# One feature block of the second token group moved from plain to paired products, in a fused retention and feed-forward kernel

## The chip, the cores and the metric

The kernel runs on one core of a Trainium2 chip. The metric is the device time of one execution in microseconds (us); the median of several runs is compared. Beside the runs there is one profiled execution, whose trace gives every instruction's start and length on each engine: PE (TensorE; PEld is its loading of stationary operands), DVE (VectorE), ACT (ScalarE), POOL (GpSimd) and SP (SyncE, which only issues transfers here).

## The reference

The input of the feed-forward part is the output of a retention block: four sequences of 768 tokens, eight heads of 64.

```python
for t in range(S):
    state = gamma * state + einsum('bhd,bhe->bhde', k[:, :, t], v[:, :, t])
    y[:, :, t] = scale * einsum('bhd,bhde->bhe', q[:, :, t], state)
x = y.transpose(0, 2, 1, 3).reshape(3072, 512)
h = x @ w_in                                   # 512 x 2048
sp = maximum(h, 0) + log1p(exp(-abs(h)))       # softplus
out = (h * erf(sp)) @ w_out                    # 2048 x 512
```

The weights arrive as 64-bit floats and are read as pairs of 32-bit words.

## The kernel before

**Tiling.** The 3072 tokens are 24 chunks of 128 (`j`), two chunks make a group of 256 (`g`, 12 of them). x of a group, transposed, is `XC[g]`: 128 partitions, 4 parts of the 512 features, 256 tokens. The 2048 hidden features are 16 blocks of 128 (`ft`), w_in comes in 8 pieces `n` of two blocks, w_out in 8 pieces as well.

**Two ways to multiply.** A *plain* product (`hidden_of`, L694) is one fp32 product of a block with one group, 4 parts deep; each shows as two matmuls of 256 columns. It needs only the converted weight. A *split* product multiplies in a rounded format: weight and x are each split into three tiles hi, lo, dif (`split_weights`, `split_x`), and three matmuls take the place of one. `unit(g, n)` (L728) does a piece's two blocks for one group, 256 columns each; `pair_unit(g, ft)` (L762) does one block for groups g and g+1 at once, 512 columns. Its sums lie in two PSUM banks `a` and `b`, which are weighted and joined: by ACT and DVE (`together`, L340 and L341), or, for the pair of groups 1 and 2 (`APART`), both are only scaled by ACT (L773, L774), stored as a high and a low part (`HID3`), and added on DVE when they are loaded again (`add_lows`, L913).

**Who is done how.** `ALONE` gives how many blocks of a group are done without a partner group: 16 of group 0, 10 of group 1, 8 of group 11. Group 0, and blocks 0 to 9 of group 1, are plain. Blocks 10 to 15 of group 1 are paired with group 2; blocks 8 and 9 of group 2 are left over and done by `unit(2, 4)`.

**Order.** The order on each engine is written out by hand; an engine takes its instructions strictly in the order in which the program issues them.

1. The retention of chunks 0 to 3 (L796 to L837), with scores, masks, products with the state, and after each chunk `A(j)` = `ret_add`: the state addition on DVE (L543) and a copy of half of the chunk's x on ACT (L536). Between them `next(weight_steps)` does single steps of the conversion of w_in to fp32: DVE takes the exponent (L235), ACT scales it (L238), DVE joins the mantissa's words (L249, L254), sets the sign (L258) and multiplies (L270). When a piece is through, its buffer is loaded again (`load_piece`, and for the first two pieces `load` of a later chunk). `need("in", ft)` does steps until block ft is converted. PE is given `keep_warm` products of the unit matrix where it would idle.
2. A loop over ft (L863): `hidden_of(ft, 0)`, `hidden_of(ft, 1)` while ft < `ALONE[1]`, the conversion two or three blocks ahead, then the items of the list `during` (the retention of chunks 4 and 5: `begin`, `states`, `results`, `crossed_sums`; splits), then `put_hidden(ft)`, which copies a bank of plain results to SBUF (ACT, L705 or L708) and stores it (POOL's queue). The plain banks are two buffers named `hp`.
3. Periods g = 2 to 11 (L1075), each a list of units with items between them: two more chunks of retention (`joined`: `begin` before one unit, `results` before another), weights split, the next chunks prepared, w_out converted in `convert` steps. `LOADS` says after which units of a period a quarter of a raw piece of w_out is loaded (POOL's queue; two buffers, so a third piece waits for the first one's last read, L258).
4. The projection (L1098): hidden values are loaded again (`load_hidden`, SP's queue), softplus, erf and product, split, and multiplied with w_out (L977). Each step n has 48 matmuls, 10.9 us.

Of the kernel before, what the change touches and what calls it, by code (L numbers as in the profile page):

```python
# [13 lines left out]
F32 = mybir.dt.float32  # L14
# [3 lines left out]
AF = mybir.ActivationFunctionType  # L18
# [3 lines left out]
P = 128  # L22
C = 128
JPC = 4
GT = 256
# [19 lines left out]
Z = 2.0**-12  # L45
# [4 lines left out]
def kernel(  # L50
# [23 lines left out]
    DH = d_model // 2  # L74
    FIRST = JPC // 2 - 1

    ALONE = {0: n_ft, 1: 5 * n_ft // 8, NG - 1: n_ft // 2}
    assert D == 64 and d_model == H * D and n_k == HP == 4 and S % GT == 0 and NJ % 2 == 0
    assert H == 8 and n_ft == 16 and NC > JPC and GT == 2 * C

# [11 lines left out]
    def b4(name, shape, dtype=F32):  # L92
        return big.tile([P] + shape, dtype, name=name, tag="b4")
# [334 lines left out]
    psum_turn = itertools.cycle((ps_r, ps_h))  # L428


    idle = ps_o.tile([P, P], F32, name="o0")

    def keep_warm(n):
        for _ in range(n):
            nc.tensor.matmul(idle, ident, ident, start=True, stop=True)

    keep_warm(7)

# [247 lines left out]

    def hidden_of(ft, g):

        bank, col = (ft, g) if ft < ALONE[1] else (ft - ft % 2, ft % 2)
        if bank not in HP_:  # L690
            HP_[bank] = ps_h.tile([P, 2, GT], F32, name="hp")
        w = WF[ft // 2].rearrange("p h a f -> p (h a) f")
        for kk in range(n_k):
            nc.tensor.matmul(  # L694
                HP_[bank][:, col],
                w[:, kk, ft % 2 * P : (ft % 2 + 1) * P], XC[g][:, kk],
                start=(kk == 0), stop=(kk == n_k - 1),
            )

    def put_hidden(ft):  # L700
        if ft >= ALONE[1] and ft % 2 == 0:
            return
        h = b2("h", [2, GT])
        if ft >= ALONE[1]:
            nc.scalar.copy(h, HP_.pop(ft - 1))  # L705
            nc.gpsimd.dma_start(HID[0][:, ft - 1 : ft + 1], h)
            return
        nc.scalar.copy(h, HP_.pop(ft))  # L708
        for g in range(2):
            nc.gpsimd.dma_start(HID[g][:, ft], h[:, g])  # L710
# [8 lines left out]
        names = [f"o{2 * own + i}" if pool is ps_o else "hp" if pool is ps_h else "r" for i in range(2)]  # L719
        return [pool.tile([P, 2, GT], F32, name=name) for name in names]  # L720

    def unit(g, n):

        a, b = banks(g == NG - 1)
        for to, parts in ((a, (0, 1)), (b, (2,))):
            for u in range(2):
                for kk, i in itertools.product(range(n_k), parts):
                    nc.tensor.matmul(  # L728
                        to[:, u],
                        W[n][i][:, kk * 2 * P + u * P : kk * 2 * P + (u + 1) * P],  # L730
                        X[g][i][:, kk],
                        start=(u == 0 and kk == 0 and i == parts[0]),
                        stop=(kk == n_k - 1 and i == parts[-1]),
                        skip_group_check=True,
                    )
        def put():
            if g not in ALONE:
                h = b4("h", [2, 2, GT])
                nc.scalar.activation(h[:, :, 0], a, AF.Copy, scale=1 + 1 / Z)
                nc.scalar.activation(h[:, :, 1], b, AF.Copy, scale=-1 / Z)  # L740
                for u in range(2):
                    nc.gpsimd.dma_start(HID3[FIRST][:, 2 * n - NPC + u, :, place_of(FIRST, g)], h[:, u])
                return
            h = b2("h", [2, GT])
            together(h, a, b)
            nc.gpsimd.dma_start(HID[g][:, 2 * n - NPC : 2 * n - NPC + 2], h)

        return put

    def place_of(g, of):  # L750

        return int(of % 3 > min(g % 3, (g + 1) % 3))
# [81 lines left out]
    ret_out(JPC - 1, lambda: hidden_of(0, 0), state_last=True)  # L834
    need("in", 1)
    hidden_of(1, 0)
    A(JPC - 1)  # L837


# [39 lines left out]
    def load_hidden(n):  # L879

        if n >= NG * NU:
            return
        HID_[n] = b4("hid", [4, GT])
        g, i = divmod(n, NU)
        of = g if g % 2 == i // 2 else g - 1
        LOWS[n] = []
        four, both = slice(i % 2 * 4, i % 2 * 4 + 4), FIRST <= of < NG - 1
        if of in APART:

            own = place_of(of, g)  # L890
            for f in range(2):
                at = slice(four.start + 2 * f, four.start + 2 * f + 2)
                if g == of and 8 + at.start < ALONE[g]:
                    src = HID[g][:, 8 + at.start : 8 + at.stop]
                else:
                    src = HID3[of][:, at, 0, own]
                    LOWS[n].append((f, b2("low", [2, GT])))
                    nc.sync.dma_start(LOWS[n][-1][1], HID3[of][:, at, 1, own])
                nc.sync.dma_start(HID_[n][:, 2 * f : 2 * f + 2], src)
        elif both:  # L900
            nc.sync.dma_start(HID_[n], HID2[of][:, four, place_of(of, g)])
        else:
            nc.sync.dma_start(HID_[n], HID[g][:, i * 4 : i * 4 + 4] if g < 2 else HID[g][:, four])
# [4 lines left out]

    def add_lows(k):
        for n in (2 * k, 2 * k + 1) if k < NH else ():  # L910
            for f, low in LOWS.pop(n):
                x = HID_[n][:, 2 * f : 2 * f + 2]
                nc.vector.tensor_tensor(x, x, low, op=ALU.add)  # L913

    def softplus(k):
# [87 lines left out]
        }  # L1003


    LOADS = {4: (3, 4, 5, 6), 5: range(2, 8), 6: (0, 1, 4, 5, 6, 7), 7: (2, 3, 4, 5), 8: (1, 2, 3, 4)}

    vals = values(2 * JPC)

    def period(g, prep, next_prep):  # L1010

        a, b = 2 * g + 2, 2 * g + 3
        one, two = partial(partial, unit), partial(partial, pair_unit)
        if g == G2:
            units = [one(g, 4)] + [two(1, ft) for ft in range(ALONE[1], n_ft)]
            return units, joined(3, 5, g), {
                0: [(hi_of, 6)],
                1: [(split_weights, 6)],
                2: [(hi_of, 7)],
                3: [(states, a), (states, b), (split_weights, 7)],  # L1020
                4: [(hi_of, 0), (split_weights, 0)],
                5: [(crossed_sums, a), (crossed_sums, b), (split_x, a, 2)],
                6: [(hi_of, 1), (split_weights, 1), (steps, next_prep, 1)],
            }, range(4)
        if g < NG:
            units = [two(g - 1, ft) for ft in range(8 - 8 * (g % 2), 16 - 8 * (g % 2))]
        if g == G2 + 1:
            return units, joined(3, 5, g), {
                0: [(steps, vals), (hi_of, 2), (steps, prep, 1)],
                1: [(steps, prep, 1), (steps, vals)],  # L1030
                2: [(split_weights, 2), (hi_of, 3)],
                3: [(states, a), (states, b), (split_weights, 3)],
                5: [(crossed_sums, a), (crossed_sums, b), (split_x, a, 2)],
                7: [(steps, next_prep, 1)],
            }, range(4)
        if g < NG - 2:
            return units, joined(2, 5, g), {
                0: [(steps, prep, 4)],
                1: [(convert, 2)],
                2: [(states, a), (convert, 1)],  # L1040
                3: [(states, b), (convert, 1)],
                4: [(convert, 2 if g < 8 else 1)],
                5: [(crossed_sums, a), (crossed_sums, b)],
                6: [(split_x, a, 2)],
                7: [(steps, next_prep, 1 if g < NG - 3 else 4), (convert, 1)],
            }, LOADS.get(g, ())
        if g == NG - 2:
            return units, joined(1, 3, g), {
                0: [(steps, prep, 4), (load_w_out, 0)],
                1: [(states, a), (load_w_out, 1)],  # L1050
                2: [(states, b), (split_w_out, 0)],
                3: [(crossed_sums, a), (crossed_sums, b)],
                4: [(split_w_out, 1), (load_hiddens, 0)],
                5: [(split_x, a, 2)],
                6: [(softplus, 0), (load_w_out, 2)],
                7: [(erf, 0), (gated, 0)],
            }, ()
        if g == NG - 1:
            return units, {}, {
                0: [(split_g, 0), (split_w_out, 2), (load_w_out, 3)],  # L1060
                1: [(split_g, 1), (load_hiddens, 1)],
                2: [(split_w_out, 3)],
                3: [(softplus, 1), (load_w_out, 4)],
                4: [(erf, 1)],
                5: [(split_w_out, 4), (load_w_out, 5)],
                6: [(gated, 1)],
                7: [(split_g, 2), (load_hiddens, 2)],
            }, ()
        return [one(NG - 1, n) for n in range(NPC // 2, NPC)], {}, {
            0: [(split_w_out, 5), (load_w_out, 6)],  # L1070
            1: [(split_g, 3), (load_w_out, 7)],
            2: [(split_w_out, 6)],
        }, ()
# [92 lines left out]
```

## Time and profile before

| what | us |
|---|---|
| runs, median (lowest to highest of 3) | 609.08 (608.69 to 610.02) |
| the profiled execution, its own time | 609.44 |
| its span, first to last instruction | 607.7 |
| busy in the span: PE / PEld | 601.1 / 503.4 |
| busy in the span: DVE / ACT / POOL | 463.0 / 395.1 / 132.3 |

The span has four stretches: retention of the first chunks to 26 us, plain blocks to 75.5 us, periods of units to 343 us, the projection to the end. The busiest lines of PE:

```profile
L762 PE MATMUL o<-x_hi,w_hi 128*128 128x512 f32 x296 | 117.4, 397 | 0.0
L977 PE MATMUL o<-w_hi,g_hi 128*128 128x512 f32 x120 | 46.7, 389 | 0.0
L694 PE MATMUL hp<-xT,w 128*128 128x256 f32 x208 | 46.3, 381 | 0.0
```

Read: line, engine, operation, result and operands, size of the stationary operand and of the result, how many, then busy time in us, the mean length of one in ns, and the engine's idle time before them. A matmul's length reaches to its modelled end and overlaps the next one; the distance between starts is what it costs when PE is fed. The mean granted TensorE clock is 0.999.

### The profile page before, as it was taken

Reading aid. Unit: us, or ns where it says so; the run is one execution under the profiler, and the core shown is the slowest. Engines: PE = TensorE matmul, PEld = TensorE weight load, DVE = VectorE, ACT = ScalarE, POOL = GpSimd, SP = SyncE. Lnnn points to the kernel's source line nnn. Section 1 sums busy time; section 2 is a strip of 40 time slices with the busy share of each in tenths; the row PEclk is TensorE's granted clock in tenths of the full one; section 3 lists DMA queues with packets and bytes.
Section 4 is the critical chain, followed back from the end, with each engine's and each line's share of the span. In section 5 each row is a group of like instructions: output and inputs, shape, how many; then the busy total and the mean of one; then the engine's idle time right before and its main releaser. Section 6 shows DMA issues by size and latency. Waiting matters only on the chain.

```text
span 607.7 us, 13134 instructions
## 1 busy us (share of the span) xinstructions
PE 601.1 (99%) x5174; PEld 503.4 (83%) x5174; DVE 463.0 (76%) x579; ACT 395.1 (65%) x620; POOL 132.3 (22%) x223
## 2 busy tenths in 40 slices
PE   8999999999999999999999999999999999999997
PEld 7888888888888888888888988888888888888886
DVE  5899898777978779787778995887777768668540
ACT  3684858354453544445487788889889888988920
POOL 1086563243536435242112200000000000000000
PEclk9999999999999999999999999999999999999999
DMA  9999698988969998795655937145424433531300
GB/s 201 305 279 269 159 259 249 248 183 241 244 177 292 262 261 189 240 234 157 204 161 186 306 127 236 47 133 174 138 70 139 146 103 99 173 126 48 105 35 35
DMA packets 147692, 109.93 MB, mean 181 GB/s; under 512 B 103152, under 2 KB 127472, under 8 KB 147632
## 3 DMA queue, kind: packets, MB, share of 16 engines
q1 hardware_dynamic: 131536, 59.93, 39.1%
q0 software_dynamic: 15536, 49.04, 25.4%
q8 instruction: 40, 0.66, 0.5%
q10 hardware_dynamic: 560, 0.14, 0.1%
q14 instruction: 20, 0.16, 0.1%
HBM read 71.58 MB, written 37.49 MB: 179 GB/s over the span
## 4 chain that ended last, share of the span: by engine, by line
PE 96%; SPq 2%; DMA 1%; ACT 0%; DVE 0%; issue 0%; DVEq 0%
PE o L762 34%; PE o L977 21%; PE r L977 11%; PE hp L977 11%; PE hp L694 8%; PE o L728 1%; DMA raw<-in_moe_w_in_dram 1%; PE hp L590 1%; PE hp L762 1%; PE r L762 1%; PE r L639 1%; PE hp L639 1%; PE r L590 1%; PE r L650 1%; PE r L597 1%; SPq L141 1%
## 5 line engine op out<-in xcount | busy, mean ns | idle before, releaser
L762 PE MATMUL o<-x_hi,w_hi 128*128 128x512 f32 x296 | 117.4, 397 | 0.0
L762 PE MATMUL o<-x_lo,w_lo 128*128 128x512 f32 x296 | 115.4, 390 | 0.0
L340 ACT ACTIVATE h<-o 128x512 f32<-128x512 f32 x70 | 41.5, 596 | 91.3 <-PE o L762 88.0
L932 DVE TENSOR_TENSOR e<-hid,e 128x1024 f32<-128x1024 f32 x48 | 56.6, 1222 | 55.6 <-ACT e L922 55.6
L762 PE MATMUL o<-x_dif,w_dif 128*128 128x512 f32 x296 | 79.1, 389 | 0.0
L341 DVE SCALAR_TENSOR_TENSOR h<-o,h 128x512 f32<-128x512 f32 x70 | 47.8, 687 | 30.9 <-ACT h L340 26.3
L779 POOL DMA_DIRECT2D hids<-h x72 | 39.7, 552 | 130.7 <-DVE h L341 129.7
L762 PEld LDWEIGHTS o<-x_hi,w_hi 128*128 128x128 f32 x296 | 55.5, 188 | 12.4
L762 PEld LDWEIGHTS o<-x_dif,w_dif 128*128 128x128 f32 x296 | 55.6, 188 | 11.6
L762 PEld LDWEIGHTS o<-x_lo,w_lo 128*128 128x128 f32 x296 | 55.6, 188 | 11.0
L334 DVE SCALAR_TENSOR_TENSOR g_dif<-g_hi,g_lo 128x1024 fp32r<-128x1024 f32 x48 | 58.8, 1225 | 3.3
L332 ACT ACTIVATE g_hi<-e 128x1024 fp32r<-128x1024 f32 x48 | 51.0, 1063 | 14.9 <-DVE e L932 12.4
L333 DVE TENSOR_TENSOR g_lo<-e,g_hi 128x1024 fp32r<-128x1024 f32 x48 | 58.7, 1222 | 0.1
L918 ACT ACTIVATE e<-hid 128x1024 f32<-128x1024 f32 x48 | 48.4, 1054 | 0.9 <-DVE hid L913 0.7
L922 ACT ACTIVATE e<-e 128x1024 f32<-128x1024 f32 x48 | 48.3, 1054 | 0.3
L977 PE MATMUL o<-w_hi,g_hi 128*128 128x512 f32 x120 | 46.7, 389 | 0.0
L977 PE MATMUL o<-w_lo,g_lo 128*128 128x512 f32 x120 | 46.7, 389 | 0.0
L977 PE MATMUL o<-w_dif,g_dif 128*128 128x512 f32 x120 | 46.7, 389 | 0.0
L694 PE MATMUL hp<-xT,w 128*128 128x256 f32 x208 | 46.3, 381 | 0.0
L694 PEld LDWEIGHTS hp<-xT,w 128*128 128x128 f32 x208 | 39.0, 190 | 5.3
L574 ACT ACTIVATE v<-v,kq_s 128x64 f32<-128x64 f32 x144 | 35.8, 342 | 0.0
L918 ACT ACT_TABLE_LOAD x24 | 30.8, 1283 | 3.4 <-DVE hid L913 1.9
(211 smaller groups left out, 1252.3 us busy)
## 6 DMA issues: line engine op xcount, KB each, us to landing
hids<-h POOLq DMA_DIRECT2D x72, 256.0 KB, 4.2
hid<-hids SPq DMA_DIRECT2D x36, 512.0 KB, 5.0
raw<-in_moe_w_in_dram SPq DMA_DIRECT2D x32, 256.0 KB, 5.3
raw<-in_moe_w_out_dram POOLq DMA_DIRECT2D x32, 256.0 KB, 6.3
out_dram<-y SPq DMA_DIRECT2D x23, 256.0 KB, 2.3
kb<-in_k_dram SPq DMA_DIRECT2D x144, 32.0 KB, 3.9
v<-in_v_dram POOLq DMA_DIRECT2D x18, 256.0 KB, 6.2
kn<-in_k_dram POOLq DMA_DIRECT2D x18, 256.0 KB, 6.8
```

Source lines behind the costliest of these rows:

```text
L332: nc.scalar.activation(hi, x, AF.Copy, scale=KEEP)
L333: nc.vector.tensor_tensor(lo, x, hi.bitcast(F32), op=ALU.subtract)
L334: nc.vector.scalar_tensor_tensor(dif, hi.bitcast(F32), Z, lo.bitcast(F32), op0=ALU.mult, op1=ALU.subtract)
L340: nc.scalar.activation(to, a, AF.Copy, scale=1 + 1 / Z)
L341: nc.vector.scalar_tensor_tensor(to, b, -1 / Z, to, op0=ALU.mult, op1=ALU.add)
L694: nc.tensor.matmul(HP_[bank][:, col], w[:, kk, ft % 2 * P : (ft % 2 + 1) * P], XC[g][:, kk], start=(kk == 0), stop=(kk == n_k - 1),)
L762: nc.tensor.matmul(to, W[n][i][:, kk * 2 * P + u * P : kk * 2 * P + (u + 1) * P], XR[i][:, at, kk], start=(kk == 0 and i == parts[0]), sto ...
L779: nc.gpsimd.dma_start(HID2[g][:, ft % 8], h)
L918: nc.scalar.activation(E[n], HID_[n], AF.Softplus)
L922: nc.scalar.activation(E[n], E[n], AF.Erf)
L932: nc.vector.tensor_tensor(E[n], HID_.pop(n), E[n], op=ALU.mult)
L977: nc.tensor.matmul(Y[g][t][x // 2], G[n][x][:, f, t * P : (t + 1) * P], W_OUT[ft // 2][x][:, ft % 2 * d_model : (ft % 2 + 1) * d_model], s ...
```

## The change

It does five things. `ALONE[1]` becomes 9, so block 9 of group 1 is paired with group 2 (`pair_unit(1, 9)`), `unit(2, 4)` keeps only its first block (`both=False`), and period g = 2 has eight units instead of seven with its items shifted by about one; `load_hidden` handles a pair of blocks of which one is plain. Two conversion steps (of piece 1) are issued ahead of `A(3)`. `keep_warm` makes one product of up to four widths of the unit matrix instead of up to four products. The quarters of raw w_out are loaded after later units (`LOADS`).

```diff
-    ALONE = {0: n_ft, 1: 5 * n_ft // 8, NG - 1: n_ft // 2}
+    ALONE = {0: n_ft, 1: n_ft // 2 + 1, NG - 1: n_ft // 2}
...
-    idle = ps_o.tile([P, P], F32, name="o0")
+    idle = ps_o.tile([P, 4, P], F32, name="o0")
...
     def keep_warm(n):
-        for _ in range(n):
-            nc.tensor.matmul(idle, ident, ident, start=True, stop=True)
+        for i in range(0, n, 4):
+            m = min(4, n - i)
+            nc.tensor.matmul(
+                idle[:, :m], ident, ident[:, None, :].to_broadcast([P, m, P]), start=True, stop=True
+            )
...
     def hidden_of(ft, g):
-        bank, col = (ft, g) if ft < ALONE[1] else (ft - ft % 2, ft % 2)
+        bank, col = (ft, g) if ft <= ALONE[1] else (ft - ft % 2, ft % 2)
...
     def put_hidden(ft):
-        if ft >= ALONE[1] and ft % 2 == 0:
+        if ft > ALONE[1] and ft % 2 == 0:
             return
         h = b2("h", [2, GT])
-        if ft >= ALONE[1]:
+        if ft == ALONE[1]:
+            nc.scalar.copy(h[:, 0], HP_.pop(ft)[:, 0])
+            nc.gpsimd.dma_start(HID[0][:, ft], h[:, 0])
+            return
+        if ft > ALONE[1]:
             nc.scalar.copy(h, HP_.pop(ft - 1))
...
-    def unit(g, n):
+    def unit(g, n, both=True):
...
-            for u in range(2):
+            for u in range(2 if both else 1):
...
             if g not in ALONE:
-                h = b4("h", [2, 2, GT])
-                nc.scalar.activation(h[:, :, 0], a, AF.Copy, scale=1 + 1 / Z)
-                nc.scalar.activation(h[:, :, 1], b, AF.Copy, scale=-1 / Z)
-                for u in range(2):
-                    nc.gpsimd.dma_start(HID3[FIRST][:, 2 * n - NPC + u, :, place_of(FIRST, g)], h[:, u])
+                h = b2("h", [2, GT])
+                nc.scalar.activation(h[:, 0], a[:, 0], AF.Copy, scale=1 + 1 / Z)
+                nc.scalar.activation(h[:, 1], b[:, 0], AF.Copy, scale=-1 / Z)
+                nc.gpsimd.dma_start(HID3[FIRST][:, 2 * n - NPC, :, place_of(FIRST, g)], h)
                 return
...
     need("in", 1)
     hidden_of(1, 0)
+    next(weight_steps)
+    next(weight_steps)
     A(JPC - 1)
...
             for f in range(2):
                 at = slice(four.start + 2 * f, four.start + 2 * f + 2)
-                if g == of and 8 + at.start < ALONE[g]:
-                    src = HID[g][:, 8 + at.start : 8 + at.stop]
-                else:
-                    src = HID3[of][:, at, 0, own]
-                    LOWS[n].append((f, b2("low", [2, GT])))
-                    nc.sync.dma_start(LOWS[n][-1][1], HID3[of][:, at, 1, own])
-                nc.sync.dma_start(HID_[n][:, 2 * f : 2 * f + 2], src)
+                k = max(0, ALONE[of] - 8 - at.start) if g == of else 0
+                if k:
+                    nc.sync.dma_start(HID_[n][:, 2 * f : 2 * f + k], HID[g][:, 8 + at.start : 8 + at.start + k])
+                at = slice(at.start + k, at.stop)
+                to = slice(2 * f + k, 2 * f + 2)
+                LOWS[n].append((to, b2("low", [2 - k, GT])))
+                nc.sync.dma_start(LOWS[n][-1][1], HID3[of][:, at, 1, own])
+                nc.sync.dma_start(HID_[n][:, to], HID3[of][:, at, 0, own])
...
-    LOADS = {4: (3, 4, 5, 6), 5: range(2, 8), 6: (0, 1, 4, 5, 6, 7), 7: (2, 3, 4, 5), 8: (1, 2, 3, 4)}
+    LOADS = {
+        4: (4, 5, 6, 7), 5: (2, 3, 4, 5), 6: (0, 1, 2, 3, 5, 6, 7), 7: (0, 3, 4, 5, 6), 8: (2, 3, 4, 5),
+    }
...
         if g == G2:
-            units = [one(g, 4)] + [two(1, ft) for ft in range(ALONE[1], n_ft)]
-            return units, joined(3, 5, g), {
+            units = [one(g, 4, False)] + [two(1, ft) for ft in range(ALONE[1], n_ft)]
+            return units, joined(4, 6, g), {
                 0: [(hi_of, 6)],
-                1: [(split_weights, 6)],
-                2: [(hi_of, 7)],
-                3: [(states, a), (states, b), (split_weights, 7)],
-                4: [(hi_of, 0), (split_weights, 0)],
-                5: [(crossed_sums, a), (crossed_sums, b), (split_x, a, 2)],
-                6: [(hi_of, 1), (split_weights, 1), (steps, next_prep, 1)],
+                2: [(split_weights, 6), (hi_of, 7)],
+                4: [(states, a), (states, b), (split_weights, 7)],
+                5: [(hi_of, 0), (split_weights, 0)],
+                6: [(crossed_sums, a), (crossed_sums, b), (split_x, a, 2)],
+                7: [(hi_of, 1), (split_weights, 1), (steps, next_prep, 1)],
             }, range(4)
```

More of the change, by code (lines that the diff above doesn't have):

```diff
@@ L910, in add_lows @@
         for n in (2 * k, 2 * k + 1) if k < NH else ():
-            for f, low in LOWS.pop(n):
-                x = HID_[n][:, 2 * f : 2 * f + 2]
+            for at, low in LOWS.pop(n):
+                x = HID_[n][:, at]
                 nc.vector.tensor_tensor(x, x, low, op=ALU.add)
```

## The prediction

> **What bounds the kernel now.** I read the totals and the chain first. TensorE (PE) is busy 99% of the span and makes up 96% of the chain that ended last.
>
> ```profile
> span 607.7 us, 13134 instructions
> PE 601.1 (99%) x5174; PEld 503.4 (83%) x5174; DVE 463.0 (76%) x579; ACT 395.1 (65%) x620; POOL 132.3 (22%) x223
> PE 96%; SPq 2%; DMA 1%; ACT 0%; DVE 0%; issue 0%; DVEq 0%
> ```
>
> A busy PE need not be a fed one, so next the chain in order of time (start, length, what).
>
> ```profile
> 11.25 5.66 DMA raw<-in_moe_w_in_dram
> ...
> 17.47 0.72 ACT power L238
> ...
> 39.46 6.91 PE hp L694 x32
> ...
> 75.86 2.87 PE o L728 x24
> 78.73 5.47 PE o L762 x24
> ```
>
> Up to 17 us a transfer of raw w_in sets the end; from about 19 us on only PE stands in the chain. The starts of PE's matmuls keep one cadence from there to 604 us: 0.216 us in plain blocks (6.91/32), 0.120 in `unit` (2.87/24), 0.227 in `pair_unit` (5.47/24, between starts a hair less). The first after a change of shape is followed about 0.1 us late. So DVE, ACT, POOL and the queues matter only where they make PE wait, and PE instructions count in full.
>
> **The change, part by part.** Durations are of the profiled execution, 609.44 us (span 607.7), which is 0.36 above the median of the runs, 609.08.
>
> *Features.* The second group's tenth block, `hidden_of(9, 1)`, goes: 4 fp32 products, two recorded matmuls each, 8 x 0.216 = -1.73. `unit(2, 4)` halves: 12 x 0.120 = -1.44. `pair_unit(1, 9)` comes: 12 x 0.227 = +2.72. Changes of shape stay as many. Together -0.44 us. [...] The trace has 0.227 in every `pair_unit`, and that row decides.
>
> *Evictions, stores and reloads.* ACT loses 2 x 0.24 on the halved `unit` (0.60 for 512 columns, 0.37 for 256) and 0.2 on block 9, and gains 2 x 0.60; POOL has the same number of stores, less one; the reload of blocks 8 and 9 of group 1 becomes three SP transfers instead of one, with one more low half of 256 columns, a DVE addition near 0.42 us (128x256 at L543). That addition has more than a projection step, 10.9 us, before PE wants its result. All zero. Without that cover each would cost its own time, 0.4 us at most.
>
> *Period g = 2.* It has eight units, not seven, and the splits and chunk steps keep their distance to the units that read them (`begin` to `results` two units, weights 6 and 7 two units before use). The new second unit wants x_lo of group 1 at about 75.6 us on the old time axis with PE's 1.73 taken off; L333 delivers it at 74.67. Zero, with 0.9 us of cover.
>
> *Raw w_out loads.* Fewer wait for a buffer that is still being read (POOL waited 8.9 us for L258 in total). Each piece is still issued four units, some 11 us, before its first step, against 6.3 us to landing. POOL's waits are not on PE's path: zero. DVE would be blocked from some 4 us of lateness on (11 less 6.3).
>
> *Dummies.* 22 recorded matmuls become 8 over the same 11 x 128 columns. The first seven products took 3.36 us, and PE then idled 0.31 until DVE was ready; the pairs are followed by an idle 0.28. A lost or gained 0.3 is hidden there, and the chain is with the DMA until 16.91 anyway. Zero, bounds -0.3 to +0.3.
>
> *Conversion steps ahead of `A(3)`.* This edit can cost. Before, `A(3)` comes first: a state addition on DVE (L543), then the copy of half of chunk 3's x on ACT (L536). DVE, then ACT:
>
> ```profile
> 24.47 0.69 DVE L270 SCALAR_TENSOR_TENSOR w<-w,power 128x512 f32<-128x512 f32 x1
> 26.35 0.42 DVE L543 TENSOR_TENSOR state<-state,o 128x256 f32<-128x256 f32 x1 [1.19 <-PE o L530]
> 26.69 0.42 DVE L235 TENSOR_SCALAR power<-raw 128x512 uint32<-128x512 uint32 x1
> 27.02 0.42 DVE L249 TENSOR_SCALAR w<-raw 128x512 uint32<-128x512 uint32 x1
> 27.48 0.69 DVE L254 SCALAR_TENSOR_TENSOR w<-w,raw 128x512 f32<-128x512 uint32 x1
> 28.09 0.42 DVE L235 TENSOR_SCALAR power<-raw 128x512 uint32<-128x512 uint32 x1
> ```
>
> ```profile
> 26.81 0.37 ACT L536 COPY xT<-o 128x256 f32<-128x256 f32 x1 [0.52 <-DVE state L543]
> 27.14 0.72 ACT L238 ACTIVATE power<-power,below 128x512 uint32<-128x512 uint32 x1
> 28.54 0.72 ACT L238 ACTIVATE power<-power,below 128x512 uint32<-128x512 uint32 x1 [0.68 <-DVE power L235]
> ```
>
> The two moved steps are the four DVE rows from L235 to the second L235 and both ACT rows L238; they issue no DMA. They fill DVE's idle 1.19 us, but L543 and L536 now queue behind them, and behind L536 stands PE: `hidden_of(0, 1)` reads this x first. It is due when `hidden_of(1, 0)`, begun at 26.23, is through: 26.23 + 0.32 + 7 x 0.216 = 28.06. DVE is free at 25.16, but piece 1's last quarter, issued at 19.88, lands 6.0 us later:
>
> ```profile
> DMA to landing us min/median/max: 6.0/6.0/6.0
> ```
>
> So at 25.92 and L235 at 26.02 (0.10 after landing, as with the first raw piece). The second L235 follows 1.40 later (26.69 to 28.09) at 27.42, its L238 0.45 later (28.09 to 28.54) at 27.87, L536 0.63 after that (one L238 of 0.72 with the overlap seen at 17.47 to 18.10), 28.50 to 28.87; PE restarts 0.03 later at 28.90. That is 0.84 late, and 0.1 at the restart makes 0.9 us. The gain of the edit is nothing: the conversions PE reads next have 1.7 us or more in hand (block 2 done at 29.83, read at 31.5). Bounds: 0, if the piece landed by 25.1, and 1.9 if a further microsecond late. I take +0.9, the row.
>
> **Sum**: -0.44 + 0.9 = +0.46 us: 609.9 against the profiled execution, 609.5 against the median. Some 0.2% (1.2 us) is what a measurement of this kernel can tell from no change, so this is no change.
>
> **Rivals.**
>
> *A, no stall.* If piece 1 lands 0.9 us sooner than in this one execution, DVE starts at 25.16, L536 ends near 28.0, PE never waits: -0.44, 608.6. For it: the landing before came at 24.15 and the following ones every 0.68 us, so 25.92 is an outlier by 1.1. Against: the next rival's rows explain the outlier by something that stays.
>
> *B, the program's own transfers move, faster.* In 14.4 to 15.7 us and again in 22 to 24.3 us the DMA view has one packet of 16 KB of another queue:
>
> ```profile
> q8 instruction: 1, 0.02, 5.5%
> ```
>
> The page has 40 of them; 10,348 PE instructions over 40 is 259 each, so they follow PE's count. The second precedes the late landing at 25.92, the first the raw transfer at 11.25 that took 5.66 us where the one before took 4.6. With 28 PE instructions fewer (14 matmuls, 14 weight loads) the first comes some 0.5 us later, past that transfer, which would land up to 1.1 us sooner. PE then waits for chunk 3's keys (landed 17.86): transposed at 18.35, copied at 18.96, scores at 19.1 instead of 19.57, 0.47 us won: -0.44 - 0.47 = -0.9, 608.2; at most -1.5. [...] Against: the second packet, 28 instructions later, waits for the state addition that ends at 22.75, and so still falls ahead of piece 1; then the stall above eats what the start won.
>
> *C, slower: ACT's copies of the plain blocks.* PE reaches blocks 10 to 15 1.73 us sooner, while ACT runs there without a gap from 64.54 us:
>
> ```profile
> 64.54 0.72 ACT L238 ACTIVATE power<-power,below 128x512 uint32<-128x512 uint32 x1 [0.89 <-DVE power L235]
> 65.17 1.04 ACT L332 ACTIVATE x_hi<-xT 128x1024 fp32r<-128x1024 f32 x1
> 66.12 0.57 ACT L708 COPY h<-hp 128x512 f32<-128x512 f32 x1
> ```
>
> Block 12 needs the bank that this L708 empties: at 66.49 with the half shape (0.37), and PE comes at 61.78 + 0.10 + 24 x 0.216 = 67.07 instead of 68.80. It decides from 0.6 us of lateness; block 14 behind L705 has 0.7. If ACT or DVE hold PE back there, the whole 1.73 is waited out: +0.46 + 1.73 = +2.2, 611.3. Against: the x they wait for comes from PE itself, so both shift together.
>
> *D, the dummies do not do it.* Fewer of them over equal columns, nothing gained or lost: this is inside the forecast.
>
> **How the numbers follow.** Forecast 0.52, A 0.20, B 0.12, C 0.16. The forecast alone: 609.0 to 610.3 (stall 0.4 to 1.4, and the runs' own scatter). The range goes to half of B below and most of the way to C above: 608.1 to 611.0. Slower by over 0.2% (above 610.3): all of C and the stall's upper end, 0.21. Faster by over 0.2% (below 607.9): the deep end of B and scatter, 0.09. Within: 0.70.
>
> **What would show it.** In the chain: L694 x200, L728 x84 in all and 12 more L762 columns of work; PE's idle time before the second eight of L694 near 28 us, ended by ACT xT L536, with L536 behind two L238; no PE wait between 62 and 76 us (else C); the first raw transfer landing before 16 us (else not B). The forecast is wrong if that wait is absent, or if any later gap of PE exceeds 0.5 us.

## The result and the profile after

| what, us | before | after |
|---|---|---|
| runs beside each other, median (lowest to highest of 22) | 609.03 (608.50 to 610.86) | 610.54 (609.23 to 619.29) |
| ratio of after to before, 95% interval | | 1.0024 [1.0017, 1.0031] |
| the profiled execution, its own time | 609.44 | 610.31 |
| its span | 607.7 | 608.3 |
| start of PE's last matmul | 603.72 | 603.93 |

The changed kernel is slower by 0.24%, some 1.5 us: just over what can be told from no change. The prediction was 609.5 and no change; the measured 610.54 lies 1 us above, inside its range of 608.1 to 611.0 but above the 609.0 to 610.3 of its forecast alone, and part of its reasons fail. Single executions far above the others of their kernel (619.29 here, 1009.58 of after_merged and 621.21 of features_dummies below) are disturbed; they are in no ratio, and no time is read from their traces.

Totals and chain of the changed kernel, then its plain blocks, the first of its `unit` rows and of its `pair_unit` rows (line, engine, operation, names, shapes, how many | busy us, mean ns | idle before). Line 694 before is L698 now, 728 is L736, 762 is L769, 590 and 597 are L594 and L601.

```profile
span 608.3 us, 13092 instructions
PE 600.6 (99%) x5152; PEld 500.4 (82%) x5152; DVE 463.1 (76%) x580; ACT 395.0 (65%) x622; POOL 131.3 (22%) x222
PE 96%; SPq 2%; DMA 1%; issue 0%; ACT 0%; DVE 0%; DVEq 0%
```

```profile
L769 PE MATMUL o<-x_hi,w_hi 128*128 128x512 f32 x300 | 118.9, 396 | 0.0
...
L698 PE MATMUL hp<-xT,w 128*128 128x256 f32 x200 | 44.6, 381 | 0.0
L736 PE MATMUL o<-x_hi,w_hi 128*128 128x256 f32 x20 | 5.1, 292 | 0.0
```

The work is what the prediction counted: 8 plain matmuls fewer (208 to 200), four of each kind of `unit` fewer (24 to 20), four of each kind of `pair_unit` more (296 to 300). PE is busy 0.5 us less, yet the execution is 0.9 us longer. So something other than work was added; totals can't show it, but the distance between the same events of both traces does.

| at | after minus before, us | what came in between |
|---|---|---|
| start of the burst at 50.6 us | -0.28 | the start |
| start of the burst at 84 us | -0.73 | the features: -0.45 |
| start of the burst at 131 us | -1.03 | before's burst at 115 us lasted 0.3 us longer |
| start of the burst at 183 us | -1.03 | nothing |
| end of that burst | +0.34 | it lasts 3.39 us instead of 2.02 |
| last matmul | +0.21 | small waits before only |
| end of the span | +0.57 | 4.34 us from the last matmul's start to the end instead of 3.98 |
| the execution's own time | +0.87 | what lies outside the span: 2.05 instead of 1.75 |

A *burst* is what `begin` (L594, L601) or `results` (L643, L654) issues at once: 128 products of 64 x 64 with 128 weight loads, 256 PE instructions in 2.02 us. The one at 183 us, in the chain of waits of the kernel before and then of the changed kernel (start, length, what):

```profile
183.80 0.62 PE hp L590 x32
184.42 0.47 PE hp L597 x32
184.89 0.47 PE r L590 x32
185.36 0.47 PE r L597 x32
185.82 1.36 PE o L762 x5
```

```profile
182.99 0.41 PE hp L594 x28
183.39 0.47 PE hp L601 x32
183.86 0.47 PE r L594 x32
184.33 0.45 PE r L601 x29
184.78 1.05 issue
185.83 0.33 PE r L601 x3
186.16 2.04 PE o L769 x8
```

Three products before the burst's end PE stops for 1.05 us and waits for nothing that the profile shows (`issue`). The stretch from 183 to 185 us holds one packet of the queue whose 40 packets the prediction found to follow PE's count. The profile gives their kind as `instruction`; taking them for PE's code is the author's reading, and they are called code packets here:

```profile
q8 instruction: 1, 0.02, 3.4%
```

It went from 183.33 to 184.41, and PE resumed at 185.83, 1.42 us after its end. Counted through the trace (matmuls, weight loads and PE's semaphore instructions), the matmul that resumes is PE instruction 193 modulo 256. Before, the burst at 115 us has a gap of 0.21 us at 194 modulo 256, with PE resuming 1.50 us after a packet's end. The two places are PE instructions 2754 (before) and 4545 (after), 1791 instructions and seven packets apart: 255.9 to a packet, and 256 is taken as a block. So a block of code seems to end there, and these waits to be PE running out of code; the experiments test it.

The time adds up. PE passed the boundary ahead of the burst (again 193 modulo 256) at 182.15. The packet started 1.18 us later, took 1.08, and PE resumed 1.42 after it: 3.68 us, and PE had used up the block between the two boundaries 2.4 us after the first. In the kernel before the packet of the same number started at 174.84, 3.6 us ahead of that boundary, and PE never waited for it.

The stall that the prediction put near 28 us isn't there. ACT's rows of that stretch, changed kernel:

```profile
25.63 0.37 ACT L539 COPY xT<-o 128x256 f32<-128x256 f32 x1 [0.72 <-PE o L526]
25.90 1.47 ACT L238 ACTIVATE power<-power,below 128x512 uint32<-128x512 uint32 x2
27.27 0.35 ACT L540 COPY xT<-o 128x256 f32<-128x256 f32 x1
```

L540, the copy that PE waits for, does stand behind two L238, but it ends at 27.62, ahead of the 27.79 at which `hidden_of(1, 0)` is through, because piece 1's last quarter landed at 24.11 and not at 25.92. It was issued 0.6 us sooner and took 1.2 us less to land. The code packets have moved, the first from 14.49 to 15.21, the second from 22.13 to 23.99. In the twelve traces used here the quarter lands at 24.94 to 25.93 where the second packet starts by 22.8 us (four traces) and at 23.84 to 24.52 where it starts after 23 (eight). They go together; no run moves that packet alone. The chain's start has changed too:

```profile
12.30 5.72 DMA kq<-in_k_dram
18.02 0.04 issue
18.06 0.45 PE r L475 x2
```

The raw transfer that set the start before (landing at 16.91) now lands at 15.46, and the last keys take its place. The first packet does not explain this: in four other kernels it started at 14.37 to 14.65, as before, and the transfer landed at 15.40 to 15.84 (steps_only, features_only, features_merged, merged_first_wide). The 16.91 belongs to the one profiled execution of before.

### The profile page after: what moved, and what is told of

It is laid out like the page before. It is cut to its first block, busy times and chain, and to the rows that moved or that the text cites. A ratio compares the mean times of both kernels' runs of the same rounds, so it can differ in the third digit from the quotient of the medians.

```text
span 608.3 us, 13092 instructions
## 1 busy us (share of the span) xinstructions
PE 600.6 (99%) x5152; PEld 500.4 (82%) x5152; DVE 463.1 (76%) x580; ACT 395.0 (65%) x622; POOL 131.3 (22%) x222
## 4 chain that ended last, share of the span: by engine, by line
PE 96%; SPq 2%; DMA 1%; issue 0%; ACT 0%; DVE 0%; DVEq 0%
PE o L769 34%; PE o L987 21%; PE r L987 11%; PE hp L987 11%; PE hp L698 7%; PE o L736 1%; DMA kq<-in_k_dram 1%; PE hp L594 1%; PE hp L769 1%; PE r L769 1%; SPq L141 1%; PE r L643 1%; PE r L601 1%; PE hp L643 1%; PE r L594 1%; PE r L654 1%
## 5 line engine op out<-in xcount | busy, mean ns | idle before, releaser
L769 PE MATMUL o<-x_hi,w_hi 128*128 128x512 f32 x300 | 118.9, 396 | 0.0
L769 PE MATMUL o<-x_lo,w_lo 128*128 128x512 f32 x300 | 116.9, 390 | 0.0
L769 PE MATMUL o<-x_dif,w_dif 128*128 128x512 f32 x300 | 80.2, 389 | 0.0
L769 PEld LDWEIGHTS o<-x_hi,w_hi 128*128 128x128 f32 x300 | 56.3, 188 | 12.5
L769 PEld LDWEIGHTS o<-x_dif,w_dif 128*128 128x128 f32 x300 | 56.3, 188 | 11.7
L769 PEld LDWEIGHTS o<-x_lo,w_lo 128*128 128x128 f32 x300 | 56.3, 188 | 11.2
L698 PE MATMUL hp<-xT,w 128*128 128x256 f32 x200 | 44.6, 381 | 0.0
L698 PEld LDWEIGHTS hp<-xT,w 128*128 128x128 f32 x200 | 37.4, 190 | 5.2
```

The costliest lines, as they stand in the source:

```text
L698: nc.tensor.matmul(HP_[bank][:, col], w[:, kk, ft % 2 * P : (ft % 2 + 1) * P], XC[g][:, kk], start=(kk == 0), stop=(kk == n_k - 1),)
L769: nc.tensor.matmul(to, W[n][i][:, kk * 2 * P + u * P : kk * 2 * P + (u + 1) * P], XR[i][:, at, kk], start=(kk == 0 and i == parts[0]), sto ...
```

## The experiments

All times are medians of runs alternating with runs of the kernel before on one chip. Before was 609.12 in the first series (the first four kernels below), 609.04 in the second (the next four), 609.07 in the third.

| kernel | median | ratio to before [95%] | PE instructions from a block boundary to the burst at 183 us | packet's start against that boundary, us | wait there, us |
|---|---|---|---|---|---|
| before | 609.03 | 1 | 45 | -3.6 | 0 |
| the changed kernel | 610.54 | 1.0024 [1.0017, 1.0031] | 3 | +1.2 | 1.27 |
| steps_only | 609.81 | 1.0012 [1.0001, 1.0023] | 45 | -3.8 | 0 |
| dummies_only | 609.02 | 0.9998 [0.9990, 1.0007] | 17 | -3.9 | 0 |
| after_old_loads | 610.97 | 1.0037 [1.0016, 1.0058] | 3 | -4.0 | 0 |
| after_pad44 | 610.46 | 1.0025 [1.0016, 1.0034] | 47 | -2.9 | 0 |
| before_one_dummy | 614.10 | 1.0081 [1.0064, 1.0097] | 5 | +1.9 | 1.70 |
| features_only | 608.74 | 0.9996 [0.9988, 1.0005] | 31 | -3.6 | 0 |
| features_merged | 608.38 | 0.9992 [0.9983, 1.0002] | 31 | -3.5 | 0 |
| after_merged | 610.27 | 1.0020 [1.0011, 1.0029] | 3 | - | - |
| features_dummies | 611.00 | 1.0034 [1.0021, 1.0048] | 3 | - | - |
| after_no_steps | 611.95 | 1.0047 [1.0030, 1.0065] | 3 | +1.1 | 1.59 |
| after_again | 610.92 | 1.0039 [1.0023, 1.0055] | 3 | +1.8 | 2.11 |
| merged_first_wide | 608.48 | 0.9998 [0.9989, 1.0007] | 11 | -4.6 | 0 |

The boundary is taken at PE instruction 193 modulo 256. The fifth column has the start of the packet that brings the next block: minus is ahead of PE's passing the boundary, plus behind. The wait is the gap between two starts. PE waits in this burst in every trace in which the packet started behind the boundary, and in none in which it started ahead of it.

**The conversion steps alone** (steps_only).

```diff
     hidden_of(1, 0)
+    next(weight_steps)
+    next(weight_steps)
     A(JPC - 1)
```

> The kernel before with the two conversion steps ahead of A(3) and nothing else. As predicted (the stall): PE waits some 0.9 us near 28 us for ACT's L536, time +0.9 (ratio 1.0015). If the transfer of piece 1 lands by 25.1 us in this build: 0. No theory expects a change of PE's waits after 100 us, since PE's instructions are the same in number and place.

Measured +0.7 us. In this execution the first code packet starts at 14.65, near its place before, the second at 20.95, and piece 1 lands at 25.13. ACT, then PE:

```profile
25.67 0.72 ACT L238 ACTIVATE power<-power,below 128x512 uint32<-128x512 uint32 x1
27.07 0.72 ACT L238 ACTIVATE power<-power,below 128x512 uint32<-128x512 uint32 x1 [0.68 <-DVE power L235]
27.70 0.35 ACT L536 COPY xT<-o 128x256 f32<-128x256 f32 x1
```

```profile
25.65 1.99 PE L694 MATMUL hp<-xT,w 128*128 128x256 f32 x8
28.10 2.21 PE L694 MATMUL hp<-xT,w 128*128 128x256 f32 x9 [0.46 <-ACT xT L536]
```

PE restarts at 28.10, 2.97 us after the landing (the prediction's working has 28.90 for 25.92, 2.98), and the gap between starts is 0.83 instead of 0.22, with 0.1 more at the restart: a stall of 0.72 us. The forecast's mechanism exists; what failed was the belief that it would meet a late piece in the changed kernel. Its bound "0, if the piece landed by 25.1" is too generous here: PE began `hidden_of(1, 0)` at 25.65 and not at 26.23, so it was due sooner too.

**The wide dummies alone** (dummies_only: `keep_warm` as in the changed kernel, nothing else).

> The kernel before with the wide dummy products and nothing else: PE's instructions behind them move 28 places forward. Theory 1 (PE's code comes in blocks of 256 instructions; a block boundary just ahead of a dense burst of 64x64 matmuls leaves 2 us to fetch the next block, and PE waits): the first fetch moves from 14.5 to about 15.2 us, the first raw transfer lands before 16 us, -0.3 at the start; late waits change with the new places: burst near 220 us starts within 5 places of a boundary, so up to +1 us there. Together -0.3 to +1. Theory 2 (the later raw loads delay the fetch): -0.3 and no new wait.

No change in the time: the prediction's zero. The code packets move (to 15.14 and 24.63), the first raw transfer lands at 15.42, and the trace is 0.33 us ahead at 50 us, as both theories had it. But features_merged and merged_first_wide, whose first packet starts at 14.57 and 14.44, are 0.38 and 0.39 ahead there: the start's gain isn't shown to come from the packets, and the median doesn't have it. The burst near 220 us starts at a boundary here and has no wait, against what theory 1 allowed; its packet started 3.7 us ahead.

**The changed kernel with the old loads of raw w_out** (after_old_loads: `LOADS` as before).

> The changed kernel with the raw w_out loads at their old places. Theory 1: the wait of 1.4 us in the burst near 183 us stays, +1.5 against before (ratio 1.0024). Theory 2: it goes, -0.7 against before (ratio 0.9988).

As slow as the changed kernel, with runs from 608.45 to 616.80. The later loads aren't what costs. The profiled run was the fastest of its twelve and has no wait at 183 us, though the burst is 3 instructions past a boundary: so the wait isn't in every execution. In the stretch from 177.9 to 179.3 us, 4 us ahead of the boundary, stands the packet:

```profile
q8 instruction: 1, 0.02, 5.8%
```

**The changed kernel with 44 more PE instructions in the first period** (after_pad44: eleven 64 x 64 products of the unit matrix, issued where ft is 1).

> The changed kernel with 11 tiny products of the unit matrix at ft = 1 (44 PE instructions, some 0.4 us), which put every later PE instruction back where it stood against the blocks of 256 in the kernel before, while the start keeps its gain. Theory 1: the wait near 183 us goes, -0.3 against before (ratio 0.9995, -1.8 against the changed kernel). Theory 2: the wait stays, +1.9 (ratio 1.003).

The wait at 183 us is gone, but the padding itself cost 1.03 us, more than the 0.4 it was thought to, and the median is 1.3 us above before where -0.3 was expected. The trace agrees with theory 1; the time isn't explained by it, and the run is inconclusive by itself.

**The kernel before, with one wide dummy** (before_one_dummy).

```diff
-        for _ in range(n):
-            nc.tensor.matmul(idle, ident, ident, start=True, stop=True)
+        for i in range(0, n, 4):
...
-    keep_warm(7)
+    keep_warm(4)
...
-    keep_warm(2)
...
-    keep_warm(2)
```

> The kernel before, with one wide dummy product of 4 x 128 columns where it had eleven of 128: PE has 40 instructions fewer ahead of everything (10 products of two recorded matmuls and two weight loads each), nearly the shift of the changed kernel (42), with no change of features, conversion order, loads or transfers. Theory 1 (PE waits where a boundary of its 16 KB code blocks falls into or just behind a burst of 256 short products, because such a burst uses up a block in 2 us): bursts at 183, 107 and 263 us now begin 5, 12 and 20 instructions past a boundary, as in the changed kernel (3, 10 and 18), so waits of some 1 us appear there; by that +1.0 us or more, 610.0 and above, and the first code fetch comes later, as in the changed kernel. Rival (the time was lost through the features, the reloads or the loads): the dummies alone do nothing, -0.3 to +0.3, no wait of PE over 0.5 us in these bursts.

+5.1 us, with nothing of the change's features in it. The wait stands at the same end of the same burst, instruction 193 modulo 256, 1.45 us after the packet's end:

```profile
185.10 0.62 PE hp L594 x32
185.72 0.47 PE hp L601 x32
186.19 0.47 PE r L594 x32
186.66 0.45 PE r L601 x28
187.11 1.48 issue
188.59 0.33 PE r L601 x3
```

In the bursts at 12 and 20 past a boundary there is none, a miss of that part. And a second cost appeared, which was expected by neither theory: PE ran the first scores at half speed.

```profile
8.31 0.21 PE r L487
...
12.87 0.10 PE r L487
```

Its scores start 0.21 us apart until 9.4 us and 0.107 apart from 12.6 on; the kernel before has 0.107 from 7.5 us. The granted clock in the profile's rows reads 1.00 throughout, so the slowness shows in the starts alone. The burst at 50.63 us came at 52.11, 1.48 us late. So with 4 of the dummies' 11 x 128 columns the first scores ran at half the pace; with all of them in wide products (dummies_only) the scores are 0.107 apart from 7.08 us on, and the time is 609.02. The profiled execution is the fastest of its six (612.42, 3.4 above before), so the rest of the 5.1 isn't accounted for by a trace.

**The features alone** (features_only: the changed kernel less the steps, the wide dummies and the new loads).

> The changed kernel with the old order of conversion steps, the old dummies and the old loads of raw w_out; the features alone. PE's instructions shift by some 14 against the kernel before. Theory 1: the work is 0.44 us less, the end costs 0.36 more (two more SP transfers, so the last output's semaphore is early in SP's list of final waits and six more waits follow it): about -0.1 us, ratio 0.9999, with single waits where a boundary happens to meet a burst. Rival (features, stores and reloads themselves cost the time): +1 us or more. Last matmul to the end: 4.34 us.

-0.3 us, with 4.34 us from the last matmul's start to the end, as expected. The profiled execution (610.21, the highest of its eleven) has one PE wait of 0.92 us at 106 us, not of the code's making:

```profile
105.06 1.22 DVE L556 TENSOR_TENSOR qb<-qb,kq_b 128x1024 f32<-128x1024 f32 x1 [3.54 <-DMA qb<-in_q_dram]
```

DVE stood for a late 32 KB load of queries, and the bank behind it came free late. after_no_steps has the same for a load of keys (3.96 us, and PE's starts 1.69 apart). The traces with the old features have no such wait, nor have the two of the changed kernel. Why SP is late there wasn't tried.

**The features with one transfer for group 2's high parts** (features_merged).

```diff
                 LOWS[n].append((to, b2("low", [2 - k, GT])))
                 nc.sync.dma_start(LOWS[n][-1][1], HID3[of][:, at, 1, own])
-                nc.sync.dma_start(HID_[n][:, to], HID3[of][:, at, 0, own])
+                if g == of:
+                    nc.sync.dma_start(HID_[n][:, to], HID3[of][:, at, 0, own])
+            if g != of:
+                nc.sync.dma_start(HID_[n], HID3[of][:, four, 0, own])
```

> The same, and the high parts of group 2's blocks come back in one transfer for each piece, so SP starts two transfers fewer and the last output has the last semaphore of SP's final list again. Theory on the end: last matmul to the end 3.97 us instead of 4.34, so 0.37 us less than the features alone, about -0.45 us against the kernel before. Rival: the end's length has another cause (the longer span of the last store, the tail's own work), and stays 4.34.

608.38, 0.36 below the features alone, and the end takes 3.98 us again. The changed kernel's +0.36 there is the price of two more transfers on SP: its last instructions are ten waits for the transfers' semaphores, in the same order in the traces of before and of the changed kernel, and before the last output (landed at 606.78) had the last one, passed at 606.80. In the changed kernel it landed at 606.99 and had the fourth, passed at 607.00. From the last output's landing to the end it is 0.91 us before and 1.27 in the changed kernel, with six more waits of 0.06 us. This is the fastest kernel of the study: 2.2 us under the changed one, its interval against the kernel before just holding 1. At 183 us:

```profile
182.64 0.62 PE hp L590 x32
183.27 0.47 PE hp L597 x32
183.74 0.47 PE r L590 x32
184.20 0.47 PE r L597 x32
```

The burst goes through without a wait.

**The same transfer in the changed kernel** (after_merged: the diff of features_merged on it).

> The changed kernel with the same one transfer for the high parts. Theory on the end: 0.37 us less than the changed kernel, +1.1 us against the kernel before; last matmul to the end 3.97 us. PE's instructions are as many as in the changed kernel, so theory 1 has waits at the same places, behind the bursts near 183 us and perhaps 107 and 263 us; the rival (one-off waits) has none there or at others.

610.27, 0.27 below the changed kernel's 610.54 of another series, within the intervals: it agrees and doesn't show it. What lies outside the span is 2.03 us in the median of the changed kernel's runs and 1.73 here, which no theory had.

**Features and wide dummies together** (features_dummies: features_only with the changed `keep_warm`).

> Two parts of the change together: the features and the wide dummies; conversion steps and raw w_out loads as in the kernel before. Alone the features measured -0.3 us (608.74 against 609.04) and the dummies nothing (609.02 against 609.03). Theory 1 (alignment of PE's code blocks with the bursts): together they shift PE's instructions by 42, so the bursts near 183, 107 and 263 us start 3, 10 and 18 past a boundary, and PE waits there: +0.7 to +1.5 us against the kernel before, with a wait of over 1 us behind the burst at 183 us. Rival (the parts add up): -0.3, no such wait.

Alone the two parts measured -0.3 and -0.1; together they measure +1.9 us, more than the 0.7 to 1.5 expected, and the fastest execution of both (610.21) lies 1.9 above the fastest of the features (608.29). So the parts don't add up. The burst's distance from a block boundary doesn't add up like times do: 14 and 28 instructions fewer leave the burst 31 and 17 past a boundary, 42 fewer leave it 3 past. The one trace, of the execution of 621.21 us, has PE stop at the same instruction, 193 modulo 256, with the packet behind the boundary. But it also has PE wait for DVE's load of keys near 109 us, as after_no_steps has, so how much of the +1.9 is code isn't shown.

**The changed kernel without the conversion steps** (after_no_steps).

> The changed kernel without the two conversion steps ahead of A(3); the shift of PE's instructions stays 42. Theory 1: as the changed kernel, -0.2 to +0.2 against it, since the steps cost nothing once piece 1 lands at 24.1 us. Rival (the stall of the steps, 0.72 us where they were put in alone, is in most executions of the changed kernel, though its profile does not show it): 0.7 us less than the changed kernel.

611.95, 1.0 above the changed kernel of the same series (610.92) where -0.2 to +0.2 was expected: a miss. It isn't 0.7 less, as the rival had it. But the profiled execution (612.65) has the late load of keys at 105 us, which neither trace of the changed kernel has; whether the other executions have it isn't known, so this run can't price the steps. PE stops again at 193 modulo 256:

```profile
186.30 0.45 PE r L601 x29
186.76 1.37 issue
188.12 0.33 PE r L601 x3
```

**The changed kernel again** (after_again, unaltered).

> The changed kernel unaltered, for a second trace of it beside the other two. Theory 1: again a wait of 1 us or more at the end of the burst near 183 us, at the same PE instruction (193 modulo 256). Rival (the wait was a single late transfer): PE waits at another place or nowhere, at the same time of some 610.5 us. No stall of PE near 28 us if piece 1 lands by 25.1 us.

610.92, and the wait in the same place: 2.11 us between starts, resumed 1.41 us after the packet's end (184.28 to 185.63). No stall near 28 us. This execution (613.19) shows what makes some runs longer still. Columns: stretch, its length, busy time and number of instructions of PE, PEld, DVE, ACT, POOL, granted clock, DMA share, GB/s.

```profile
186.00:187.00 1.00, 0.00 (x0) 0.00 (x0) 0.97 (x2) 0.00 (x0) 1.00 (x2) 1.00 1.12 200
187.00:188.00 1.00, 0.96 (x6) 0.81 (x6) 0.00 (x0) 0.00 (x0) 0.09 (x1) 1.00 1.12 198
188.00:189.00 1.00, 1.00 (x6) 0.77 (x5) 0.00 (x0) 0.00 (x0) 0.54 (x1) 0.78 1.33 204
189.00:190.00 1.00, 1.00 (x4) 0.81 (x3) 0.00 (x0) 0.00 (x0) 0.00 (x0) 0.50 0.88 247
190.00:191.00 1.00, 1.00 (x4) 0.81 (x3) 0.00 (x0) 0.60 (x1) 0.00 (x0) 0.50 1.02 401
191.00:192.00 1.00, 1.00 (x4) 0.71 (x4) 0.17 (x1) 0.00 (x0) 0.00 (x0) 0.52 1.10 417
192.00:193.00 1.00, 1.00 (x6) 0.82 (x5) 1.00 (x3) 0.00 (x0) 0.18 (x1) 1.00 1.02 386
```

After the wait the granted clock is 0.50 for some 3.4 us, and the next burst is 14.24 us away instead of the 10.41 of before: 2.2 us by the longer burst, 1.6 by the clock.

**The merged features, with only the first seven dummies wide** (merged_first_wide).

> The features with group 2's high parts loaded in one transfer, and of the dummies only the first seven made two wide products: PE's instructions shift by 34, not 42, so the bursts at 183, 107 and 263 us start 11, 18 and 26 past a boundary, beyond the 3 to 5 at which a wait showed (at 10, 12, 18 and 20 none did). Theory 1: no wait in these bursts; -0.7 us against the kernel before as without the wide products (608.38 against 609.04), up to 0.3 more if the later first code fetch lets the raw transfer land sooner. Rival (any shift of some 30 to 40 brings the waits back): +0.5 or more.

608.48: no wait at a distance of 11, with the packet 4.6 us ahead of the boundary, and no gain over features_merged either. Its first code packets lie where they did before (14.44 and 22.71), and the trace is 0.39 us ahead of before at 50 us all the same, as features_merged is.

## Why the prediction was right or wrong

By the prediction's own signs its mechanism failed: the wait near 28 us is absent, and a later gap of PE exceeds 0.5 us (1.05 us at 184.8 in the chain). That 610.54 lies in its range is luck: the 0.9 us of a stall that didn't come stood in for costs that the sum didn't have.

- **Features, -0.44**: right, -0.45 in the trace between 50 and 84 us; no wait between 62 and 76 us, so rival C fell. The products of `pair_unit` start 0.227 us apart in the changed kernel too, and the sum rightly goes by that.
- **Evictions and reloads, zero**: wrong by 0.36. The three transfers in place of one were priced by what waits for their data, and not by the program's last instructions, ten waits for the transfers' semaphores in both traces. features_merged took it away (4.34 to 3.98).
- **Period 2 and raw loads, zero**: no wait inside the span is theirs. But what lies outside the span is 2.03 us in the median of the changed kernel's runs and 1.75 to 1.78 in those of before; with the old loads it is 1.81, with the merged transfer 1.73. So the new loads and the two transfers cost some 0.25 us together and not singly; how stays open.
- **Conversion steps, +0.9**: the mechanism and its arithmetic are right (0.72 us alone, PE back 2.97 us after the landing), but in both traces of the changed kernel the term is 0. The step that failed is in the case against rival B, that the second packet "still falls ahead of piece 1": it moved from 22.13 to 23.99 and piece 1 landed 1.8 us sooner, at 24.11. The 25.92 on which the term rests is also the latest of all traces: steps_only, the same program up to there, has 25.13, features_only 23.94. So rival A's word for it, an outlier, was partly right.
- **Dummies, zero, with D as harmless**: right alone (609.02), wrong in company. The prediction counted the code packets, 259 instructions each, and asked only which transfer they delay. It didn't ask what PE does when a burst eats a block in 2.02 us and its packet comes late, 1.2 us behind the boundary here. That is the missing term: 1.37 us in the profiled execution. features_dummies has +1.9 without the steps and the new loads, of which part may be the late load.
- **Rivals A and B**: both came true in part. There was no stall, and the first raw transfer landed at 15.46 instead of 16.91, worth 0.28 us at the start instead of 0.47, since the keys' transfer then set the end (18.02). But B's reason for it fails: with the packet at 14.37 to 14.65 that transfer lands at 15.40 to 15.84 in four other traces, so the late landing was that execution's own.
- **The sum**: -0.28 (start) - 0.45 (features) + 1.37 (code) + 0.36 (end) + 0.30 (outside the span) is +1.30; the -0.43 left are waits that before had and after hadn't. So +0.87 between two executions. The +1.5 between medians is not taken apart by a trace of a median execution; the wait in the burst was 1.27 to 2.11 us in the three traces that have it at distance 3, and absent in the fourth.

## What to carry to other kernels

In this kernel, with PE busy 99% of the span, the number of PE's instructions mattered apart from their work: 42 fewer took the burst at 183 us from 45 to 3 places past a boundary, and at 3 PE waited 1.27 to 2.11 us there in three traces of four. In a kernel like it, count from the start where each 256th instruction falls, see in the trace whether the code packet starts ahead of PE's passing that place (2.9 to 4.6 us ahead and no wait in eight traces here) or behind it (1.1 to 1.9 us behind and a wait in four), and try keeping a dense burst from beginning just behind such a place. Test parts of a change in pairs and not only alone: -0.3 and -0.1 us alone were +1.9 together here, part of it perhaps a late load. Read a landing time from several executions before a term of a forecast rests on it: 25.92 us in one was 24.11 in the changed kernel. And a transfer more can cost time even when nobody waits for its data: two more on SP's queue lengthened the end by 0.36 us.

## What the runs showed of the hardware

- The code packets were 40 of 16 KB here (41 in steps_only), with 255.9 PE instructions to a packet between the waits of before and of the changed kernel, and PE resumed 1.41 to 1.56 us after a packet's end in each of the five waits timed (0.21, 1.27, 1.59, 1.70 and 2.11 us between two starts, with four of them in the burst at 183 us). At none of the 469 boundaries (256 instructions apart) counted in twelve traces (all but after_merged and features_dummies) did PE go on sooner than 1.41 us after the end of its packet. The four waits over 1 us stand where the 256 instructions of a burst take 2.02 us without a wait and the packet started 1.1 to 1.9 us behind the boundary; with the packet 2.9 to 4.6 us ahead, in eight traces, the same burst has none.
- Bursts that start 3 or 5 instructions past a boundary waited over 1 us in four of the five traces counted; those at a boundary (dummies_only, 219.7 us) and from 10 on had no gap above 0.21 us. What goes with it is the packet: 1.1 to 1.9 us behind the boundary in those four, 4.0 ahead of it in the fifth. Why it comes late there is open.
- After PE's wait of 2.11 us (after_again) the granted clock fell to 0.50 for some 3.4 us; after 1.27 (the changed kernel), 1.59 (after_no_steps) and 1.70 us (before_one_dummy) it stayed at 1.00.
